# Score visits of three pieces in batches 1 and 2, and narrower dummy matmuls before batch 0's first scores

## The chip, the core and the metric

The kernel runs on one core of one Trainium2 chip. The core has engines that work side by side, each through its own queue in the order in which the instructions were written: TensorE (in the profile PE, with its weight loads as PEld) multiplies matrices into PSUM banks; VectorE (DVE) and ScalarE (ACT) do elementwise work and are the ones that read PSUM; GpSimd (POOL) casts and issues loads; SyncE (SP) issues loads, transposing transfers and stores. Engines wait for one another through semaphores. The metric is the time of one execution on the device in microseconds.

## The reference

Attention with a few extra "beacon" keys, then a two-layer MLP with a squared ReLU. B, H, S, D = 8, 8, 576, 64 (batches, heads, tokens, width of a head), 16 beacons, and for the MLP 4608 tokens x 512, hidden width 2048:

```python
k_all = np.concatenate([beacon_k, k], axis=2)
v_all = np.concatenate([beacon_v, v], axis=2)
scores = scale * np.matmul(q, k_all.transpose(0, 1, 3, 2))
scores = np.where(causal, -1000000000.0, scores)      # beacons are seen by all tokens
a = softmax(scores)
x = (a @ v_all), the heads of a token side by side    # 4608 x 512
h = x @ w_in
r = np.maximum(h, 0.0)
out = (r * r) @ w_out
```

The inputs and the output are float32; the kernel multiplies in bfloat16.

## The kernel before

**Work.** The eight batches run through attention one after another. In a batch two heads form a pair, four pairs in all. The scores are computed transposed (keys on the partitions, queries along the row), in blocks that leave out what the causal mask removes. For each pair 1664 columns per head are left; the four pairs of a batch are cut into 13 *pieces* of 512 columns per head (`STREAM`, `PIECES`, lines 556 to 575). A piece is computed by TensorE (line 620, the two heads on the two halves of the array's rows), put through an exponential by ScalarE into `pt` (line 629, or line 671 in halves), masked by VectorE (lines 712, 716), multiplied by v on TensorE (line 738, with a column of ones that gives the sum) and normalized by VectorE (lines 755, 757) into `xn`. `xn` is transposed into `xT`, by TensorE for batches 0 to 2 (line 805) and by DMA after that. The MLP takes tokens in nine chunks of 512: the first layer (line 901), the ReLU on ScalarE or VectorE (lines 917, 919), the square on VectorE (line 926), the second layer (line 939; line 851 at the very end), copies out of PSUM and stores. A chunk needs the attention of all its tokens: chunk 0 lies in batch 0, chunk 1 in batches 0 and 1, and so on.

**PSUM.** There are two *strips* (two banks each, a piece for both heads) and four single `ps` banks. The `ps` banks serve the MLP's products, the attention-value products, the transposes and the dummies.

**Score visits.** A *visit* is one stretch in which TensorE computes the scores of several pieces, one after the other. `PLAN` (line 636) gives the sizes of the visits of batches 1 to 7. A visit of two takes both strips. A visit of three takes both strips and two `ps` banks besides: its first piece goes into the two banks, one head each, and its exponential is run as two instructions of 512 columns (line 671); the other two pieces go into the strips and have one exponential of 1024 each (line 629). A visit of three is also written behind the visit before it (line 659). Batch 0 is computed otherwise, per pair in four smaller pieces (`add_pair`).

**Loads.** Batches 0 and 1 have q and k brought by GpSimd's DMA queue directly in bfloat16 (line 449) and transposed by TensorE (lines 481 and 484, copied out to `qT` and `kT` at line 497, by way of the helper at lines 325 and 327). Pair 0 of batch 0 comes first, over `osb`, in two parts (lines 522 and 530). The order on GpSimd's queue is a list (`SOFT`, line 976): pairs 1 to 3 of batch 0, its v, w_in in four quarters, then batch 1's q and k (two pairs at a time), v and w_out. From batch 2 on, SyncE loads, GpSimd casts and SyncE transposes by DMA (line 404).

**The order.** `Order.run` (lines 70 to 199) is a planner that runs while the program is built. Every operation has engines that it may run on, an assumed duration, a priority, dependencies, and the banks or buffers that it takes and gives. The planner runs a clock over these and, each time an engine is free, writes down the available operation of the lowest priority number. The engines later run what was written in that order. Where TensorE has nothing available in the first 22 us of the planner's clock, it writes a *dummy* matmul on zeros (lines 145 to 150, written out at line 295) of 128 or 256 columns, which the planner books at 0.107 us either way. The dummies keep TensorE at work until the first data are there.

The first scores of batch 0 need the first part of pair 0 of q and k: cast (line 530), transposed (line 481), copied out by VectorE, and the beacon keys (lines 416 to 438). In the written order the dummies and the transposes of the second part stand ahead of them.

Of the kernel before, what the change touches and what calls it, by code (L numbers as in the profile page):

```python
# [46 lines left out]
class Order:  # L47
# [22 lines left out]
    def run(self):  # L70
# [9 lines left out]
        def release(op):  # L80
            for e in op.engs:
                avail[e].append(op)
# [11 lines left out]
        now = 0.0  # L94
        while events:
            now = events[0][0]
# [18 lines left out]
            while again:  # L115
                again = False
                for e in engines:
                    if free[e] > now + 1e-9:
                        continue
                    best = None  # L120
                    fallback = None
                    held = False
                    for op in avail[e]:
                        if any(free[x] <= now + 1e-9 for x in op.engs[:op.engs.index(e)]):
                            continue
                        if op.take:
                            pool, cls, need = op.take
                            if len(self.pools[pool]) < need or held and pool == "ps":
                                continue
                            if op.wide and len(self.pools["ps"]) < 2:  # L130
                                continue
                            if cls in self.limits and self.inuse[cls] + need > self.limits[cls]:
                                continue
                        if op.gate is not None and not op.gate(self):
                            if fallback is None or op.prio < fallback.prio:
                                fallback = op
                            continue
                        if op.dma and len(lanes[e]) >= self.DEPTH[e] and lanes[e][-self.DEPTH[e]] > now + 1e-9:
                            continue
                        if best is None or op.prio < best.prio:  # L140
                            best = op
                    if best is None:
                        best = fallback
                    if best is None:
                        if e == "PE" and 0.3 < now < self.FILL_UNTIL and self.pools["ps"]:
                            cols = 128 if now < 4.0 else 256
                            free[e] = now + 0.107
                            issued.append((Op("fill", "PE", 0.107, lambda e, cols=cols, bank=self.pools["ps"][0]: self.fill(bank, cols)), e, now))
                            seq += 1
                            heapq.heappush(events, (free[e], seq, "free", None))  # L150
                        continue
                    op = best
                    started.add(id(op))
                    for u in op.followers:
                        u.left -= 1
                        if u.left == 0:
                            release(u)
                    for ee in op.engs:
                        avail[ee].remove(op)
                    if op.take:  # L160
                        pool, cls, need = op.take
                        op.slots = [self.pools[pool].pop(0) for _ in range(need)]
                        op.held = (pool, cls, op.slots[0])
                        if op.wide:
                            op.wide = [self.pools["ps"].pop(0) for _ in range(2)]
                        if cls in self.inuse:
                            self.inuse[cls] += need
                    dur = op.dur[e] if isinstance(op.dur, dict) else op.dur
                    end = now + dur
                    free[e] = end  # L170
                    self.progress += op.pe_time
                    issued.append((op, e, now))
                    seq += 1
                    heapq.heappush(events, (end, seq, "free", op))
                    if op.dma:
                        dma_free = max(dma_free, now + self.DMA_LAT[e]) + op.dma
                        seen = max(end, dma_free + 1.6)
                        lanes[e].append(seen)
                        seq += 1
                        heapq.heappush(events, (seen, seq, "free", op))  # L180
                    else:
                        seen = end + self.LAT[e]
                    seq += 1
                    heapq.heappush(events, (seen, seq, "done", op))
                    seq += 1
                    heapq.heappush(events, (seen + op.late, seq, "done_pe", op))
                    if op.give is not None:
                        seq += 1
                        heapq.heappush(events, (seen, seq, "give", op))
                    again = True  # L190
# [12 lines left out]
def kernel(  # L203
# [429 lines left out]

    exps_of = {}
    SHIFT = 0.25
    PLAN = ((2,2,2,2,2,2,1),(2,2,2,2,2,2,1),(2,3,3,3,2),(2,3,3,3,2),(2,3,3,3,2),(2,3,3,3,2),(2,3,3,3,2))
    FREE = 2
    last_qk = []

    def add_batch(b):  # L640
# [3 lines left out]
        n = 0  # L644
        for size in PLAN[b - 1]:
            pos = HP * b + 512.0 * n / PW
            box = {}
            runs = [(0,), (1, 2)] if size == 3 else [tuple(range(size))]
            for k, run in enumerate(runs):
                def emit(e, run=run, n=n, box=box, size=size):  # L650
                    for s in run:
                        if size == 3 and s == 0:
                            emit_scores(b, PIECES[n], [ps[x] for x in box["qk"].wide])
                        else:
                            st = strips[box["qk"].slots[s - (size == 3)]]
                            emit_scores(b, PIECES[n + s], [st[:, 0, :], st[:, 1, :]])

                qk = add(f"qk{b}.{n + run[0]}", "PE", 0.2 / len(runs) + 512 * len(run) / 2400.0, emit,
                         prio=-1.0e6 if k else 100.0 * pos - 1000.0, behind=[qk] if k else last_qk[-1:] if size == 3 or b > FREE else [],
                         take=None if k else ("strip", "strip", min(size, 2)), gate=None if k else gate_at(pos - SHIFT))  # L660
# [410 lines left out]
```

## Time and profile before

| | |
|---|---|
| median of 5 runs | 339.14 us (338.79 to 339.21) |
| the profiled execution | 339.21 us, span of its instructions 337.5 us |
| TensorE busy | 333.0 us (99%) |
| ScalarE, VectorE, GpSimd busy | 193.6, 164.1 and 91.7 us |
| the MLP's two layers on TensorE (lines 901, 939) | 74% of the chain that ended last |
| attention-value products (738), scores (620), dummies (295) | 9%, 8%, 3% of that chain |
| exponentials of 1024 columns and the like (629) | 92, 1004 ns each |
| exponentials of 512 columns (671) | 30, 598 ns each |
| dummies | 32 of 128 columns, 51 of 256 |

A line of the profile names the engine, the line of the kernel, the instruction, its output and inputs, shapes, how many (x12) and, in brackets, how long the engine was idle before it and whose work ended the wait. Times are microseconds from the start of the span unless marked ns. A matmul's length in the timeline includes its way through the array, which the next one overlaps; how fast a row of matmuls goes is read from where they start, or from the chain, in which each piece ends where the next begins. The score rows say `strip` or `ps` for where the result goes; in a visit of three the `ps` rows come first.

### The profile page before, as it was taken

Reading aid. Unit: us, or ns where it says so; the run is one execution under the profiler, and the core shown is the slowest. Engines: PE = TensorE matmul, PEld = TensorE weight load, DVE = VectorE, ACT = ScalarE, POOL = GpSimd, SP = SyncE. Lnnn points to the kernel's source line nnn. Section 1 sums busy time; section 2 is a strip of 40 time slices with the busy share of each in tenths; the row PEclk is TensorE's granted clock in tenths of the full one; section 3 lists DMA queues with packets and bytes.
Section 4 is the critical chain, followed back from the end, with each engine's and each line's share of the span. In section 5 each row is a group of like instructions: output and inputs, shape, how many; then the busy total and the mean of one; then the engine's idle time right before and its main releaser. Section 6 shows DMA issues by size and latency. Waiting matters only on the chain.

```text
span 337.5 us, 7825 instructions
## 1 busy us (share of the span) xinstructions
PE 333.0 (99%) x3197; PEld 188.2 (56%) x3197; DVE 164.1 (49%) x384; ACT 193.6 (57%) x290; POOL 91.7 (27%) x145
## 2 busy tenths in 40 slices
PE   8999999999999999999999999999999999999996
PEld 7578766544554555545458845554555544444444
DVE  3786977147465982477117823574247303301400
ACT  3886765377647846566567556676557216515611
POOL 9874803315404604051144032404000000000000
PEclk9999999999999999999999999999999999999999
DMA  8999989999999999899799968998210221011003
GB/s 152 194 207 219 204 145 210 224 244 210 197 206 246 172 194 182 187 232 180 144 242 242 200 134 181 247 195 152 74 62 2 45 89 62 0 64 62 0 15 113
DMA packets 143956, 51.74 MB, mean 153 GB/s; under 512 B 130703, under 2 KB 138799, under 8 KB 143919
## 3 DMA queue, kind: packets, MB, share of 16 engines
q1 hardware_dynamic: 135375, 42.19, 61.4%
q0 software_dynamic: 7904, 8.69, 15.0%
q8 instruction: 25, 0.41, 0.5%
q10 hardware_dynamic: 639, 0.36, 0.4%
q14 instruction: 13, 0.10, 0.1%
HBM read 37.22 MB, written 9.44 MB: 138 GB/s over the span
## 4 chain that ended last, share of the span: by engine, by line
PE 99%; ACT 0%; DVE 0%; issue 0%
PE ps L901 38%; PE ps L939 36%; PE ps L738 9%; PE strip L620 7%; PE ps L295 3%; PE ps L484 1%; PE ps L620 1%; PE ps L805 1%; PE ps L851 1%; PE ps L481 0%; PE ps L429 0%; ACT osb L325 0%; DVE g L301 0%; DVE warm L302 0%
## 5 line engine op out<-in xcount | busy, mean ns | idle before, releaser
L901 PE MATMUL ps<-xT,w_in 128*128 128x512 bf16 (+3 forms) x704 | 134.5, 340 | 0.0
L939 PE MATMUL ps<-w_out,g 128*128 128x512 bf16 x560 | 130.8, 379 | 0.0
L629 ACT ACTIVATE pt<-strip 128x1024 bf16<-128x1024 f32 (+3 forms) x92 | 87.4, 1004 | 22.6 <-PE strip L620 22.2
L901 PEld LDWEIGHTS <-w_in 128*128 128x128 bf16 x704 | 65.3, 98 | 51.5 <-issue 0.9
L917 ACT ACTIVATE g<-ps 128x512 bf16<-128x512 f32 (+2 forms) x119 | 66.9, 562 | 45.2 <-PE ps L901 44.5
L926 DVE TENSOR_TENSOR g<-g 128x1024 bf16<-128x1024 bf16 (+2 forms) x80 | 52.6, 665 | 67.3 <-ACT g L917 66.4
L939 PEld LDWEIGHTS <-g 128*128 128x128 bf16 x560 | 51.2, 98 | 55.8 <-issue 1.7
L327 POOL CAST qk_area<-stg 128x512 bf16<-128x512 f32 (+2 forms) x60 | 40.2, 679 | 62.5 <-DMA stg<-in_k_dram 35.3
L325 ACT COPY osb<-ps 128x512 f32<-128x512 f32 (+2 forms) x34 | 19.3, 571 | 58.0 <-PE ps L939 54.7
L327 POOL CAST vb<-stg 128x512 bf16<-128x512 f32 (+1 forms) x40 | 25.2, 638 | 71.5 <-DMA stg<-in_v_dram 53.5
L738 PEld LDWEIGHTS <-pt 128*128 128x128 bf16 (+1 forms) x960 | 36.4, 98 | 11.0 <-issue 0.6
L738 PE MATMUL ps<-vb,pt 128*128 128x65 bf16 (+1 forms) x960 | 39.4, 194 | 0.0
L712 DVE TENSOR_TENSOR pt<-pt,tri 128x512 bf16<-128x512 bf16 x64 | 28.6, 455 | 19.7 <-ACT pt L671 10.0
L757 DVE TENSOR_TENSOR xn<-ps,rcp 128x320 bf16<-128x320 f32 (+2 forms) x64 | 31.5, 492 | 2.4
L919 DVE TENSOR_SCALAR g<-ps 128x512 bf16<-128x512 f32 (+2 forms) x41 | 24.0, 603 | 14.2 <-PE ps L901 14.0
L620 PEld LDWEIGHTS <-kT 64*128 64x128 bf16 x596 | 19.4, 94 | 17.7 <-issue 16.1
L755 DVE RECIPROCAL rcp<-ps 128x5 f32<-128x5 f32 (+2 forms) x64 | 12.2, 191 | 34.7 <-PE ps L738 34.2
L620 PE MATMUL strip<-qT,kT 64*128 64x112 bf16 (+15 forms) x506 | 29.0, 239 | 0.0
L671 ACT ACTIVATE pt<-ps 128x512 bf16<-128x512 f32 x30 | 16.3, 598 | 6.4 <-PE ps L620 5.2
L327 DVE COPY osb<-ps 128x512 f32<-128x512 f32 (+1 forms) x4 | 2.4, 591 | 23.0 <-PE ps L851 11.7
L295 PE MATMUL ps<-g 128*128 128x256 bf16 (+1 forms) x83 | 11.7, 298 | 1.1 <-DVE warm L302 1.1
L371 POOL DMA_DIRECT2D stg<-in_v_dram x10 | 8.8, 886 | 5.2 <-DMA w_in<-in_moe_w_in_dram 3.8
(42 smaller groups left out, 95.2 us busy)
## 6 DMA issues: line engine op xcount, KB each, us to landing
out_dram<-osb SPq DMA_DIRECT2D x17, 512.0 KB, 4.2
stg<-in_q_dram SPq DMA_DIRECT2D x24, 256.0 KB, 5.0
stg<-in_k_dram SPq DMA_DIRECT2D x18, 256.0 KB, 4.8
stg<-in_v_dram SPq DMA_DIRECT2D x18, 256.0 KB, 4.6
w_in<-in_moe_w_in_dram POOLq DMA_DIRECT2D x4, 512.0 KB, 7.7
w_out<-in_moe_w_out_dram POOLq DMA_DIRECT2D x4, 512.0 KB, 11.2
stg<-in_v_dram POOLq DMA_DIRECT2D x6, 256.0 KB, 8.0
stg<-in_k_dram SPq DMA_DIRECT2D x6, 224.0 KB, 4.4
```

Of the source, the lines that this page charges most:

```text
L295: nc.tensor.matmul(ps[bank][:, 0:cols], g[1][:, 0, 0:128], g[1][:, 0, 0:cols], start=True, stop=True)
L327: eng[e].tensor_copy(dst, src)
L620: nc.tensor.matmul(st[hj][:, at:at + t1 - t0], kT[b % 2][hp, pr, 128 * c:128 * c + 128], qT[b % 2][hp, pr, t0:t1], start=True, stop=True,)
L629: nc.scalar.activation(pt[:, :, at:at + width], strips[qk.slots[s]][:, :, 0:width], AF.Exp, bias=0.0, scale=scale)
L712: nc.vector.tensor_tensor(out=d, in0=d, in1=tri[:, m0:m0 + m, :][:, None].to_broadcast([128, 2, m, 128]), op=ALU.min)
L738: nc.tensor.matmul(a[:, at + (t - tl[0]) * (D + 1):at + (t - tl[0] + 1) * (D + 1)], P[0:rr, hj, o:o + 128], vb[b % 2][0:rr, c, 2 * pr + hj ...
L757: nc.vector.tensor_tensor(out=xn[b % 2].rearrange("p t (h d) -> p h t d", d=D)[:, h0:h0 + nh, tl[0]:tl[0] + nt], in0=a[:, :, :, 0:D], in1= ...
L901: nc.tensor.matmul(h[:, lo - spans[0][0]:hi - spans[0][0]], w_in_sb[:, mc, ft * 128:(ft + 1) * 128], xT[:, mc, lo % RING:lo % RING + hi - lo],
L917: nc.scalar.activation(dst, h, AF.Relu, bias=0.0, scale=1.0)
L919: nc.vector.tensor_scalar(out=dst, in0=h, scalar1=0.0, scalar2=None, op0=ALU.max)
L926: nc.vector.tensor_tensor(out=d, in0=d, in1=d, op=ALU.mult)
L939: nc.tensor.matmul(o, G[:, fc, ts * 128:(ts + 1) * 128], w_out_sb[:, fc, :], start=(fc == 0), stop=(fc == NFT - 1))
```

## The change

Two numbers of the plan change. Dummies are 128 columns wide until the planner's clock reads 7.0 instead of 4.0. The visits of batches 1 and 2 become (2, 2, 3, 3, 3) instead of (2, 2, 2, 2, 2, 2, 1); the pieces are the same 13.

```diff
                         if e == "PE" and 0.3 < now < self.FILL_UNTIL and self.pools["ps"]:
-                            cols = 128 if now < 4.0 else 256
+                            cols = 128 if now < 7.0 else 256
                             free[e] = now + 0.107
...
     SHIFT = 0.25
-    PLAN = ((2,2,2,2,2,2,1),(2,2,2,2,2,2,1),(2,3,3,3,2),(2,3,3,3,2),(2,3,3,3,2),(2,3,3,3,2),(2,3,3,3,2))
+    PLAN = ((2,2,3,3,3),(2,2,3,3,3),(2,3,3,3,2),(2,3,3,3,2),(2,3,3,3,2),(2,3,3,3,2),(2,3,3,3,2))
     FREE = 2
```

## The prediction

> **What bounds the kernel now.** I read the page's busy shares and its chain first, then the chain in order of time, then TensorE's timeline of the first 10 us with the other engines' beside it, last the landing of single loads.
>
> ```profile
> PE 333.0 (99%) x3197; PEld 188.2 (56%) x3197; DVE 164.1 (49%) x384; ACT 193.6 (57%) x290; POOL 91.7 (27%) x145
> ...
> PE 99%; ACT 0%; DVE 0%; issue 0%
> ```
>
> TensorE is busy 99% of the span, and the chain that ended last is TensorE alone. So only less streaming, fewer dead spots inside its stream, or an earlier start shorten the time. The chain in order of time (start, length, what) shows the dead spots:
>
> ```profile
> 65.58 0.86 PE ps L939 x4
> ...
> 78.32 0.55 PE strip L620 x12
> ...
> 105.67 0.33 PE ps L620 x6
> 105.99 0.44 PE strip L620 x12
> ...
> 123.79 2.59 PE ps L939 x12
> ...
> 129.57 2.69 PE ps L939 x12
> ...
> 306.41 13.81 PE ps L901 x64
> ```
>
> 64 matmuls of 512 columns take 13.81, one 0.216. Twelve take 2.59 when attention-value products follow (123.79), but 2.69 when a score visit follows: entering a visit costs 0.10. A visit of two pieces takes 0.55; the two heads of a piece stream side by side, so its columns need 2 x 0.216 = 0.43, and leaving costs 0.12. A visit of three (105.67 with 105.99) takes 0.77 for 0.65 of columns: again 0.12. So **a visit costs 0.22 us beside its columns, whatever its size.**
>
> The other place is the start. TensorE's timeline, and the same rows cut at 6.28:
>
> ```profile
> 5.25 2.30 PE L295 MATMUL ps<-g 128*128 128x256 bf16 x15
> 7.38 0.46 PE L481 MATMUL ps<-ident,qk_area 112*128 112x112 bf16 x6
> 7.78 0.33 PE L620 MATMUL strip<-qT,kT 64*128 64x240 bf16 x4
> ```
> ```profile
> 5.25 1.21 PE L295 MATMUL ps<-g 128*128 128x256 bf16 x5
> ```
> ```profile
> 6.08 1.47 PE L295 MATMUL ps<-g 128*128 128x256 bf16 x11
> ```
>
> VectorE and ScalarE, the first things that follow (in brackets the idle time before):
>
> ```profile
> 7.88 0.51 DVE L327 COPY kT<-ps 128x336 bf16<-128x336 bf16 x1 [1.64 <-PE ps L481]
> ```
> ```profile
> 8.15 0.78 ACT L629 ACTIVATE pt<-strip 128x736 bf16<-128x736 f32 x1 [2.84 <-PE strip L620]
> ```
>
> Between 5.25 and 7.38 TensorE does nothing but 15 dummies. The inputs of the transposes at 7.38 were ready at 5.83 (VectorE's cast, 5.48 to 5.83), those of the first scores at 6.25 (copy of qT, 5.85 to 6.25). **The dummies themselves hold up the first scores**, and ScalarE, which then runs exponentials nearly without a pause to 18.3, starts late.
>
> **The change, part one: the dummies.** The order planner books 0.107 us for a dummy of either width, so the number and places of the dummies stay as they are; only columns change. By the planner's own durations its clock starts dummies at 0.45; 32 of them, transposes (0.27) and the beacon's (0.25) bring it to about 4.4, 15 dummies to 6.0, transposes (0.38) and first scores (0.35) to 6.73. So the 15, and some three of the four after the first scores, fall below 7.0 and shrink. The fifth dummy starts at 6.08, so four took 0.83, about 0.21 each; the eleven from 6.08 to 7.38 are one of 0.21 and ten of 0.109. The clock doubled at 6.29. (The granted clock reads 1.00 throughout; the spacing tells.) Before 4.51 the 128-column dummies came every 0.106. After the change: one at 5.25 that is followed in 0.08, as the first of all was, nine more up to 6.29, and five at half of 0.109, 0.28 in all: transposes at 6.57 instead of 7.38, **0.81 earlier**, first scores at 6.97, above the bound of 6.25. Three of the next four give 0.16 more: 0.97.
>
> The Trainium skill, "TensorE: Matmul & The Clock Gate", section "What's actually happening", says that a monitor lifts the half clock after a busy window of about 3.4 us, and that this window runs freely, so the moment differs between runs by some half a microsecond. Here the doubling comes 5.2 us after the first dummy, which fits a window that began on its own; by the rule a later moment would raise the gain of the 15 dummies towards 1.6 us, which the loads named next would cut to the same 0.5. The page's closing table ("Why this matters for your kernels") warns of idle gaps over about 3 us, after which the clock halves again, and so speaks against shorter dummies; one such window at half clock would cost about 1.7 us and turn the sum into a small loss. TensorE has no gap above 0.2 us in these rows.
>
> The 0.97 cannot all reach the end, because TensorE runs into loads that do not move (the page's DMA row stands at 8 or 9 tenths from the start to beyond 140 us). Pair 3's q of batch 0 is issued at 8.48 and lands 6.2 later, 14.7; its transposes start at 15.45, slack 0.7. Then batch 1's last q load (issued 21.17) and the transposes that need it, TensorE's timeline:
>
> ```profile
> qk_area<-in_q_dram POOLq DMA_DIRECT2D x1, 288.0 KB, 12.7
> ```
> ```profile
> 34.17 0.70 PE L484 MATMUL ps<-ident,qk_area 96*64 96x96 bf16 x24
> ```
>
> It lands at 33.83, and of these 24 the twelve of q start at 34.41, after twelve of k: slack 0.58, less 0.06 from landing to start. So **0.5 us survives**; the rest becomes a short wait there. These loads are issued by GpSimd behind w_in and wait for no matmul. Bounds: 0 (another engine takes it) and 0.97; I take 0.5, the tightest row.
>
> **Part two: the visits.** Batches 1 and 2 go from seven visits each to five: four visits fewer x 0.22 = **0.88 us** on the chain. The columns stay. The first two visits of batch 1 (33.6, 38.1) are the same as before, so the order on every queue is unchanged until about 41 us. Six visits become three-piece ones. Each replaces one exponential of 1024 (about 0.98 in a run) by two of 512 (1.08 for both, at 106.2): 0.1 x 6 = 0.6 us on ScalarE, which between 33 and 102 us is idle a third of the time or more except in 33 to 45 (9.45 of 12 busy) and 65 to 81 (11.5 of 16). Cost 0 while that idle time lasts, 0.6 without it. No DMA is added; stores and loads of SyncE and GpSimd keep their dependencies, batch 2's transposed q and k land at 70.9 against a first use at 75.0, and w_out's last quarter at 49.5 against 51.1.
>
> What is added as a wait: a three-piece visit needs both strips and two of the four ps banks free together, and must follow the visit before it. Behind it on TensorE's queue stand the first-layer blocks, which want the same banks, and on ScalarE their ReLUs, then behind 3.0 us of exponentials instead of 1.94. In batches 3 to 7 fifteen such visits stand beside the same blocks without a pause of TensorE (4.42 for 20 matmuls after 106.4). In 41 to 45 us it is tighter: VectorE is busy 10.85 of the 12 us from 33 to 45. Bound for that one visit: VectorE alone serves a block of 272 in 0.44 plus 0.2 of squaring, TensorE makes one in 0.46; over 3.0 us it falls 1.8 blocks behind, 0.85 us, if no second-layer block fills in. The other bound is 0 (24 matmuls ran through two exponentials at 38.7 in 2.88, 0.03 over their columns). I take 0.1, nearer to that row. The reordering after 41 us may also join or split neighbours: four entries at 0.1 either way, taken as 0.
>
> **Sum.** The profiled execution took 339.21 (span 337.5 and 1.7 around it): 339.21 - 0.5 - 0.88 + 0.1 = 337.9. It lies 0.07 above the median of 339.14, within the spread of 0.42.
>
> **Rivals.** (1) *The early gain is lost*, in the waits of rows 15.45 and 34.17 or on VectorE before 45; only the visits count: 339.1 - 0.88 + 0.1 = 338.4 (338.1 to 338.7). For it: VectorE's load; against it: the slack of 0.5 is there in the rows. (2) *More than forecast*: neighbours join too (0.4) or batch 0's loads land earlier: 337.3. (3) *The shorter dummies free less*, if the clock is up before 5.3: then 15 take 1.6 now and 0.8 after, the first scores come against their bound of 6.25, and 0.7 is left, still more than the 0.5 that the load lets through; where more goes, it falls in with (1). (4) *Slower: TensorE runs dry before chunk 1.* Its first matmuls (64.7) need all of batch 1's attention, and only one block of 0.86 (row 65.58) is left of chunk 0 then. The last visit of batch 1 is at 54.27 now. If three-piece visits wait long for two banks at once, it comes later, and beyond 0.86 every microsecond is idle. To end 0.2% slower it must eat 1.3 + 0.7 + 0.86, thus start after 57.1. The visits at 105.6, 110.8 and 115.2 stand 4.4 to 5.2 apart, which from 41.5 puts the last at 51 to 52, earlier than now. At 8.5 apart it would start at 58.5: 3.4 idle, 339.2 + 3.4 - 1.4 = 341.2. (5) *The same stall in small*: 1 us of it cancels most: 338.9.
>
> **How the numbers follow.** Forecast 337.9 (own range 337.4 to 338.4) 0.60; (1) with (3) 0.16, half of it over the bound; (2) 0.07; (5) 0.08, no measurable change; (4) 0.09. A measurement of this kernel tells 0.2%, 0.7 us, from no change: faster is below 338.46. Faster 0.60 + 0.09 + 0.07 = 0.76, same 0.07 + 0.07 = 0.14, slower 0.10. The range 337.2 to 339.0 leaves out (4) and the ends of (2) and (5).
>
> **What will show it.** In the changed profile: the 15 dummies end near 6.6 and the first exponential starts near 7.35; the transposes near 33.9 wait for the load; batches 1 and 2 have five visits each, the exponentials of 512 (line 671) go from 30 to 42; the chain holds no piece but TensorE's; the last visit of batch 1 lies before 54. Wrong would be: TensorE idle after 41 us, above all before chunk 1's first matmuls, or dummies that end as late as now.

## The result and the profile after

| | before | after |
|---|---|---|
| median time | 339.05 us (48 runs) | 338.13 us (27 runs) |
| ratio, 95% interval | 1 | 0.9977 (0.9968 to 0.9986) |
| span of the profiled execution | 337.5 us | 336.5 us |
| TensorE busy | 333.0 us | 331.4 us |

The kernel became 0.8 us faster by the ratio, 0.9 by the medians. The forecast was 337.9, a gain of 1.2. The sign was right and the size a third to a half too large, and one of the two parts gave next to nothing, as the profile and the experiments show. The page's chain by engine, which was TensorE alone before:

```profile
PE 89%; DMA 6%; POOL 4%; issue 0%; ACT 0%; POOLq 0%
```

Where the transfers stand in it, the chain in order of time says (start, length, what):

```profile
6.10 0.82 POOL stg L371
6.92 6.85 DMA stg<-in_v_dram
...
17.75 1.42 POOL w_in L830 x2
19.17 1.97 POOL qk_area L449 x3
21.14 13.39 DMA qk_area<-in_q_dram
34.57 0.45 PE ps L484 x12
```

Up to 34.5 us the end now hangs on GpSimd's queue and on two loads; TensorE enters the chain only with the transposes of the load that the prediction had named. TensorE's own timeline of the same execution:

```profile
5.25 1.41 PE L295 MATMUL ps<-g 128*128 128x128 bf16 x15
6.50 0.46 PE L481 MATMUL ps<-ident,qk_area 112*128 112x112 bf16 x6
6.89 0.33 PE L620 MATMUL strip<-qT,kT 64*128 64x240 bf16 x4
...
14.49 0.45 PE L484 MATMUL ps<-ident,qk_area 96*64 96x96 bf16 x12 [0.68 <-DMA qk_area<-in_k_dram]
...
33.99 1.03 PE L484 MATMUL ps<-ident,qk_area 96*64 96x96 bf16 x24
...
38.23 0.62 PE L620 MATMUL strip<-qT,kT 64*128 64x96 bf16 x12
```

The first scores come at 6.89 instead of 7.78, and the second visit of batch 0 at 8.24 instead of 9.29, 1.05 earlier. At 14.49 TensorE waits 0.68 for pair 3's k. The 24 transposes at 33.99 take 1.03 where they took 0.70, because q lands in their middle. Batch 1's second visit then starts at 38.23, where it was at 38.09 before: **the whole second won at the start is gone.** Three loads took it, each of which landed later than in the profile before:

| load | landed before | landed after | TensorE's lead behind it |
|---|---|---|---|
| (none yet; second visit of batch 0) | | | 1.05 |
| pair 3's k of batch 0 | 13.89 | 14.45 | 0.30 |
| batch 1's first k | 29.34 | 29.85 | 0.18 |
| batch 1's last q | 33.83 | 34.53 | -0.12 |

Matmul by matmul the lead falls at these three places and at no other before 38 us, and 0.75 of the 1.05 goes at pair 3's k. The rest of the span, from batch 1's second visit on, is 298.3 instead of 299.4: this is where the time was won. The rows of the profile before for it:

```profile
38.09 0.62 PE L620 MATMUL strip<-qT,kT 64*128 64x96 bf16 x12
38.64 2.95 PE L901 MATMUL ps<-xT,w_in 128*128 128x272 bf16 x24
...
64.56 1.03 PE L901 MATMUL ps<-xT,w_in 128*128 128x512 bf16 x4
65.42 1.03 PE L939 MATMUL ps<-w_out,g 128*128 128x512 bf16 x4
```

The 24 matmuls at 38.64 take 2.79 in the profile after, and as much with the dummies alone and with the wide dummies below, which have the old visits here. So 0.15 of the 1.1 is a pause that this one execution of the kernel before had. The visits of three in batch 1, TensorE's timeline after the change:

```profile
41.51 0.39 PE L620 MATMUL ps<-qT,kT 64*128 64x192 bf16 x6
41.74 0.60 PE L620 MATMUL strip<-qT,kT 64*128 64x224 bf16 x12
46.32 0.39 PE L620 MATMUL ps<-qT,kT 64*128 64x192 bf16 x4
46.55 0.61 PE L620 MATMUL strip<-qT,kT 64*128 64x144 bf16 x14
54.44 0.40 PE L620 MATMUL ps<-qT,kT 64*128 64x208 bf16 x6
54.67 0.60 PE L620 MATMUL strip<-qT,kT 64*128 64x272 bf16 x12
```

### The profile page after: what moved, and what is told of

Read it like the earlier page. It is cut to its first block, busy times and chain, and to the rows that moved or that the text cites. A ratio compares the mean times of both kernels' runs of the same rounds, so it can differ in the third digit from the quotient of the medians.

```text
span 336.5 us, 7856 instructions
## 1 busy us (share of the span) xinstructions
PE 331.4 (99%) x3197; PEld 188.6 (56%) x3197; DVE 170.4 (51%) x389; ACT 191.2 (57%) x291; POOL 92.1 (27%) x145
## 4 chain that ended last, share of the span: by engine, by line
PE 89%; DMA 6%; POOL 4%; issue 0%; ACT 0%; POOLq 0%
PE ps L939 36%; PE ps L901 36%; PE ps L738 8%; PE strip L620 5%; DMA qk_area<-in_q_dram 4%; PE ps L620 2%; DMA stg<-in_v_dram 2%; POOL qk_area L449 1%; PE ps L851 1%; POOL w_in L830 1%; POOL vb L327 1%; PE ps L805 1%; PE ps L484 0%; POOL tri L311 0%; POOL stg L371 0%; POOL stg L370 0%
## 5 line engine op out<-in xcount | busy, mean ns | idle before, releaser
L629 ACT ACTIVATE pt<-strip 128x1024 bf16<-128x1024 f32 (+3 forms) x86 | 81.4, 1004 | 13.2 <-PE strip L620 13.0
L325 ACT COPY osb<-ps 128x512 f32<-128x512 f32 (+2 forms) x29 | 16.4, 568 | 65.2 <-PE ps L939 60.5
L712 DVE TENSOR_TENSOR pt<-pt,tri 128x512 bf16<-128x512 bf16 x64 | 29.7, 472 | 12.3 <-ACT pt L629 6.7
L919 DVE TENSOR_SCALAR g<-ps 128x512 bf16<-128x512 f32 (+2 forms) x42 | 24.7, 605 | 13.2 <-PE ps L901 12.3
L671 ACT ACTIVATE pt<-ps 128x512 bf16<-128x512 f32 x42 | 22.8, 597 | 13.7 <-PE ps L620 11.1
L620 PE MATMUL strip<-qT,kT 64*128 64x208 bf16 (+13 forms) x474 | 27.0, 239 | 0.0
L327 DVE COPY osb<-ps 128x512 f32<-128x512 f32 (+1 forms) x9 | 5.8, 647 | 33.9 <-PE ps L939 22.1
L295 PE MATMUL ps<-g 128*128 128x128 bf16 (+1 forms) x83 | 10.7, 287 | 1.1 <-DVE warm L302 1.1
```

The lines of the kernel that those rows point to most:

```text
L327: eng[e].tensor_copy(dst, src)
L620: nc.tensor.matmul(st[hj][:, at:at + t1 - t0], kT[b % 2][hp, pr, 128 * c:128 * c + 128], qT[b % 2][hp, pr, t0:t1], start=True, stop=True,)
L629: nc.scalar.activation(pt[:, :, at:at + width], strips[qk.slots[s]][:, :, 0:width], AF.Exp, bias=0.0, scale=scale)
L671: nc.scalar.activation(pt[:, hj, at:at + 512], ps[qk.wide[hj]], AF.Exp, bias=0.0, scale=scale)
L712: nc.vector.tensor_tensor(out=d, in0=d, in1=tri[:, m0:m0 + m, :][:, None].to_broadcast([128, 2, m, 128]), op=ALU.min)
L919: nc.vector.tensor_scalar(out=dst, in0=h, scalar1=0.0, scalar2=None, op0=ALU.max)
```

## The experiments

Theory: up to about 50 us the stream of loads on GpSimd's queue sets the pace, so that an earlier start of TensorE only lengthens its waits; after that TensorE's own stream sets the time, and the visits shorten it. Rival A: half a microsecond of the earlier start survives. Rival B: the gain comes from the start, and the visits are paid back.

**Each part alone.** The dummies alone (this diff and those of the next three kernels are against the kernel before, the later ones against the changed kernel, and they show what is new):

```diff
-                            cols = 128 if now < 4.0 else 256
+                            cols = 128 if now < 7.0 else 256
```

> The dummies' change alone, visits as before. Theory (the loads set the pace of the first 35 us): first scores near 6.9 instead of 7.8, then TensorE waits for a load of q or k, near 14 or near 34 us, and by batch 1's second visit (38.1 before) it is no more than 0.3 us earlier; time 338.8 to 339.1, within 0.1% of before. Rival A (0.5 us of the earlier start survives, as the prediction had it): second visit at 37.6, time about 338.5, ratio 0.9985.

Ratio to the kernel before 1.0001 (0.9982 to 1.0019). Its timeline:

```profile
5.26 1.78 PE L295 MATMUL ps<-g 128*128 128x128 bf16 x15
6.83 0.59 PE L481 MATMUL ps<-ident,qk_area 112*128 112x112 bf16 x6
7.35 0.33 PE L620 MATMUL strip<-qT,kT 64*128 64x240 bf16 x4
...
16.40 0.45 PE L484 MATMUL ps<-ident,qk_area 96*64 96x96 bf16 x12 [1.01 <-DMA qk_area<-in_q_dram]
```

In this execution the clock rose later, so that all 15 dummies took 0.105 us each; the first scores still came 0.43 earlier than before, and a wait of 1.01 at 16.40 took it back. The loads were late here too, and the second visit of batch 1 starts at 39.30; this execution is one of the longer ones of its kernel (340.33, the median is 339.00). The interval of the time (0.6 us to each side) would hold rival A's 0.5 as well; it is the waits that speak against it.

The visits alone:

```diff
-    PLAN = ((2,2,2,2,2,2,1),(2,2,2,2,2,2,1),...
+    PLAN = ((2,2,3,3,3),(2,2,3,3,3),...
```

> The visits alone, dummies as before. Theory (each visit costs two changes of TensorE's row mode at 0.097, four visits fewer are eight changes fewer, 0.78, and one short pause near 40.3 goes): time 0.8 to 0.9 below before, ratio 0.9975, the same as the whole change within 0.1%. Rival A (both parts add): 0.8 below before, and the whole change 0.4 to 0.5 better than this. Rival B (the gain lies in the earlier start, visits are paid back by more work on ScalarE): ratio 0.999 to 1.000.

Ratio 0.9984 (0.9961 to 1.0007), median 338.22, within 0.1 us of the whole change; its profiled span of 336.4 and second visit at 38.16 are those of the whole change. From the second visit on it takes 298.2. TensorE waits for no load in it, and its chain is TensorE's: with the old dummies it came just in time. In these two executions the narrower dummies turned work on zeros into waiting and nothing else.

**Dummies made wider**, to move TensorE's start the other way:

```diff
-                            cols = 128 if now < 4.0 else 256
+                            cols = 128 if now < 4.0 else 512 if now < 7.0 else 256
...
-    nc.vector.memset(g[1][:, 0, 0:256], 0.0)
+    nc.vector.memset(g[1][:, 0, 0:512], 0.0)
```

> Dummies of 512 columns where the change has 128 (between 4.0 and 7.0 of the planner's clock), visits as before: TensorE's start is moved the other way. First scores near 9.5 instead of 7.8 by twice the cost per dummy (five more at the slow clock, the rest at 0.216), some 1.9 later with the three after them. Theory (elastic up to the slack before the loads, stiff beyond): of 1.9 us the slack of 0.6 is taken up, 1.2 to 1.5 reach the end; time 340.3 to 340.6, while 1 us earlier brought nothing. Rival A (start moves the end one to one): 341.0. Rival C (loads hide the start wholly): 339.1.

Ratio 1.0055 (1.0038 to 1.0072), 1.9 us longer, at the upper end of what was expected. The interval includes rival A's 341.0, and in this direction the trace sides with rival A: first scores at 9.03, 1.25 later than before, batch 0's second visit 1.56 later, batch 1's second visit at 39.66, 1.57 later, and no wait for a load. The expectation reckoned the slack of 0.6 the wrong way round. Slack before a load is eaten by being early; whoever comes later than the load pays all of it.

**Small visits in all batches:**

```diff
-    PLAN = ((2,2,2,2,2,2,1),(2,2,2,2,2,2,1),(2,3,3,3,2),...
+    PLAN = ((2,2,2,2,2,2,1),) * 7
```

> Visits of (2, 2, 2, 2, 2, 2, 1) in all seven batches: ten visits and twenty changes of row mode more than before. Theory (0.097 for each change, nothing else on TensorE's path): 20 x 0.097 = 1.9 us longer, 341.0, ratio 1.0057. Rival B (visits of three are dear in other ways, so that small ones are not worse): 339.1 or less. Rival D (small visits also bring stalls by the strips): over 342.

Ratio 1.0062 (1.0047 to 1.0076), 2.1 us for ten visits and twenty changes of the array's form: 0.10 for each change, 0.21 for a visit. Rivals B and D fall.

**One load more**, the same data fetched twice:

```diff
+                if i == 0:
+                    nc.gpsimd.dma_start(out=w_out_sb[:, 0:4, :], in_=moe_w_out.rearrange("(c p) f -> p c f", p=128)[:, 0:4, :])
                 return [nc.gpsimd.dma_start(
```

> The changed kernel with one load more on GpSimd's queue ahead of w_in (w_out's first quarter, 1 MB of float32, which is loaded again at its usual place); nothing else moves, no engine computes more. Theory (the stream of loads sets the pace up to the last of w_out, near 50 us): all later loads land about 2.5 us later (the four quarters of w_in land 2.5 to 3.3 apart), TensorE, which has no slack at batch 1's last q load, waits that long, and time rises by 2.2 to 2.7: 340.3 to 340.8. Rival A (TensorE's own stream sets the time and the waits at loads are chance): under 0.7.

Ratio to the kernel before 1.0049 (1.003 to 1.0069), which is 0.7% or 2.4 us over the changed kernel, as the theory had it, though no engine computes more and the order is the same. Its timeline (lines after 830 are shifted by two) shows where:

```profile
23.61 0.58 PE L903 MATMUL ps<-xT,w_in 128*128 128x240 bf16 x4 [0.52 <-DMA w_in<-in_moe_w_in_dram]
29.25 1.97 PE L903 MATMUL ps<-xT,w_in 128*128 128x240 bf16 x16 [0.85 <-DMA w_in<-in_moe_w_in_dram]
32.77 0.70 PE L484 MATMUL ps<-ident,qk_area 96*64 96x96 bf16 x24 [1.55 <-DMA qk_area<-in_k_dram]
```

The last q of batch 1 lands 2.9 later than after the change alone (37.44), the span is 2.7 longer and the time 2.4: a later load counts nearly in full. These seven kernels share the written order up to batch 1's second visit, and their profiled executions can be set side by side (the landing is the issue of batch 1's last q load plus its time to landing):

| kernel | q lands | second visit | landing to visit | visit to end of span |
|---|---|---|---|---|
| before | 33.83 | 38.09 | 4.26 | 299.4 |
| dummies alone | 35.60 | 39.30 | 3.70 | 299.3 |
| wide dummies | 34.59 | 39.66 | 5.07 | 299.0 |
| visits alone | 34.43 | 38.16 | 3.73 | 298.2 |
| the whole change | 34.53 | 38.23 | 3.70 | 298.3 |
| one load more | 37.44 | 41.14 | 3.70 | 298.1 |
| small visits everywhere | 34.89 | 38.60 | 3.71 | 301.2 |

In four of seven the visit starts 3.70 to 3.71 us after the landing, with the old dummies (small visits) as with the narrow ones; the visits alone, with the old dummies, touch that bound. Only where TensorE is later (before, wide dummies) does it set the time itself. The last column depends, to within 0.4, on the visits alone. And the landing moves by 1.8 us between executions whose loads are the same (without the one with a load more): the execution from which the slack of 0.58 was read had the earliest of them.

**Giving the early start somewhere to go.** If TensorE waits for batch 1's load, its transposes should stand later in the order:

```diff
-                    after = [add_part_load(b, 0, prs, x, prio + n, after, [], 1.5, 1.5)]
+                    after = [add_part_load(b, 0, prs, x, prio + n, after, [], 1.5, 3.5)]
```

> The changed kernel, with the planner told that batch 1's q and k loads are seen 2 us later (1.5 becomes 3.5): TensorE's transposes of them are written four first-layer blocks (16 matmuls, about 1.9 us) later; nothing else before them moves. Theory (after the change TensorE waits for the landing of batch 1's last q load): no wait between 29 and 36 us, three changes of row mode fewer (0.3), time 0.5 to 0.9 below the changed kernel's 338.1, about 337.4. Rival A (that load is passed anyway, the early gain goes elsewhere): only the 0.3 of the row mode, 337.8 or more.

338.28, ratio 0.9977 (0.9958 to 0.9995): no better than the change, so the expectation failed, and rival A's 337.8 or more held. The wait at 34 is gone, but others have taken its place:

```profile
10.07 0.45 PE L484 MATMUL ps<-ident,qk_area 96*64 96x96 bf16 x12 [0.78 <-DMA qk_area<-in_k_dram]
49.72 1.02 PE L939 MATMUL ps<-w_out,g 128*128 128x512 bf16 x3 [0.88 <-DMA w_out<-in_moe_w_out_dram]
```

At 10.07 TensorE stands before pair 2's k of batch 0, at 49.72 before w_out's last quarter. The same kernel with the old dummies:

> The same as the one before with the old dummies (256 columns from 4.0 on); the written order is the same. Theory: with the load at 34 us out of the way the dummies count as far as the first load, pair 3's k near 14 us, lets them: 0.2 to 0.5 us longer than with the narrow dummies, though the same pair without this edit differed by nothing. Rival A (the early start is lost somewhere else): equal. Rival E (nothing else in the way): 1.0 longer.

338.87, ratio 0.9989 (0.9973 to 1.0005). The medians differ by 0.6 from the narrow dummies, but the intervals overlap, and here w_out landed later (51.0), which again is what ended the wait. With pair 3's load moved ahead of v as well:

```diff
-    SOFT = "t0 p1k p1q t1 p2k p2q v0 v1 p3k p3q v2 v3 v4 w0 w1 w2 w3".split()
+    SOFT = "t0 p1k p1q t1 p2k p2q p3k p3q v0 v1 v2 v3 v4 w0 w1 w2 w3".split()
```

> The changed kernel with the late transposes of the first run and, besides, pair 3's k and q of batch 0 loaded ahead of v instead of behind two of its loads, so that the wait near 14 us goes too. Theory: TensorE's early second of the dummies passes both places; 0.3 to 0.8 below the late transposes alone, about 336.8. Rival F (v then lands too late for the first attention-value products, and the wait only moves): equal or slower.

337.93, ratio 0.9965 (0.9952 to 0.9979), no clear step; and with the old dummies:

> The same as the one before with the old dummies, the written order the same. Theory: with both loads out of the way the dummies are worth what they free at the start, 0.7 to 1.05 us: about 337.7 against 336.8. Rival A: equal. Rival F: a difference under 0.3, because v's landing holds both.

338.15, ratio 0.9971 (0.9957 to 0.9985). The dummies' 0.7 to 1.05 did not appear in the medians, which lie 0.2 apart. (The two profiled executions say little of it: the first scores came at 7.02 and 7.23, because the clock rose earlier in the second.) Both stand before w_out, here the kernel with the narrow dummies and then the one with the old:

```profile
49.49 1.02 PE L939 MATMUL ps<-w_out,g 128*128 128x512 bf16 x3 [0.72 <-DMA w_out<-in_moe_w_out_dram]
```
```profile
49.80 1.02 PE L939 MATMUL ps<-w_out,g 128*128 128x512 bf16 x3 [0.66 <-DMA w_out<-in_moe_w_out_dram]
```

**The last load of the stage.** In the kernel with both edits and the narrow dummies, the planner was told besides that w_out is seen late, by 4 us (5 in a second kernel):

```diff
-            w_ops["out", i] = add(..., behind=[v_loads[1][4]] if i == 0 else [w_ops["out", i - 1]], dma=2.6)
+            w_ops["out", i] = add(..., behind=[v_loads[1][4]] if i == 0 else [w_ops["out", i - 1]], dma=2.6, late=4.0)
```

> The kernel with pair 3 loaded early and batch 1's transposes late, and the planner told besides that w_out's loads are seen 4 us later. There TensorE waited 0.9 us for w_out's last quarter (landed 49.45). Theory: with that wait gone, 0.5 to 0.9 below it, 337.1 to 337.4. Rival G (the work put ahead is missing later, and TensorE waits at another place up to chunk 1's start): 337.9 or more.

> The same with 5 us instead of 4, which writes batch 1's attention-value products ahead of the second layer's first block. Theory: 337.1 to 337.4 as with 4. Rival G: 337.9 or more.

340.68 and 341.02, ratios 1.0043 (1.0026 to 1.0061) and 1.0054 (1.0036 to 1.0072): slower than the kernel before, as rival G had it. The first of them:

```profile
59.76 0.39 PE L620 MATMUL ps<-qT,kT 64*128 64x208 bf16 x6
...
63.44 0.43 PE L805 MATMUL ps<-ident,xn 112*128 112x112 bf16 x5 [0.95 <-DVE xn L757]
64.30 1.27 PE L738 MATMUL ps<-vb,pt 128*128 128x65 bf16 x30 [0.43 <-DVE pt L712]
66.54 0.43 PE L805 MATMUL ps<-ident,xn 112*128 112x112 bf16 x5 [0.97 <-DVE xn L757]
66.81 6.44 PE L901 MATMUL ps<-xT,w_in 128*128 128x512 bf16 x27
```

The last visit of batch 1 slid to 59.76, and before chunk 1 (66.81) TensorE ran dry three times, 2.35 us together. This is the mechanism of the prediction's fourth rival, brought about by another cause. With 2 us instead of 4 the planner writes one other block between, and the visits hardly move:

> The kernel with pair 3 loaded early and batch 1's transposes late, and w_out's loads taken to be seen 2 us later instead of 4: the block that needs w_out's last quarter is written 1.3 us later, the visits of batch 1 at most 0.9 later. Theory: the wait for w_out (0.7 to 0.9 there) goes and, as the last visit of batch 1 stays before 54.4, no wait takes its place before chunk 1: ratio to the kernel before 0.994 to 0.995, about 337.2. Rival G (as with 4 and 5 us, TensorE runs dry before chunk 1): 0.997 or more.

337.21, **ratio 0.9949 (0.9932 to 0.9966), span 334.9**, better than both kernels: its interval ends just below that of the change. Between 5 and 75 us one wait of TensorE is left:

```profile
10.81 0.45 PE L484 MATMUL ps<-ident,qk_area 96*64 96x96 bf16 x12 [0.18 <-DMA qk_area<-in_k_dram]
...
51.51 0.40 PE L620 MATMUL ps<-qT,kT 64*128 64x208 bf16 x6
...
63.54 2.75 PE L901 MATMUL ps<-xT,w_in 128*128 128x512 bf16 x12
```

The last visit starts at 51.51 and chunk 1 at 63.54. Before the change a block of chunk 0's second layer still stood behind chunk 1's first block (the row at 65.42 above); here none is left, so that like for like chunk 1 comes 1.9 earlier. Not all of this is the early start: the late transposes save three changes of the array's form besides, about 0.3. No run with the old dummies stands beside this kernel, so what the narrow ones are worth in it is not shown.

## Why the prediction was right, and where it was not

*The total.* 337.9 against 338.1 is in part luck. The sum held a gain of 0.5 from the start, 0.88 from the visits and a loss of 0.1. In the profiled executions the start gave -0.1 and everything behind batch 1's second visit 1.1. A term that did not come was half made up by one that came out larger and by a loss that did not show. The sign "the chain holds no piece but TensorE's" failed too: 6% of it are loads and 4% GpSimd.

*The visits, 0.88.* Right: five visits in each of the two batches, 42 exponentials of 512 columns instead of 30, and the price of 0.22 per visit held: 0.21 from the small visits everywhere, and 0.7 to 1.3 from the last column of the table for four visits (299.0 to 299.4 against 298.1 to 298.3). Eight changes of form at 0.10 are 0.8 of it, and 0.15 of the difference between the profiles before and after is the pause at 38.64; the rest was not traced. The Trainium skill, "TensorEngine Tiling (Array Packing)", section "Key Properties", says that changing the tiling mode drains TensorE, without a figure. The runs put a change at 0.10 us each way; that draining is the cause no run here shows.

*The start, 0.81 and 0.97.* Right as far as it goes: 0.89 and 1.05 in the profile after. The moment of the clock is not fixed. The dummies' spacing puts it at 6.29 before, near 6.15 after, later than 6.83 with the dummies alone, near 7.0 with the late transposes and the old dummies, and in the profile of the small visits the first 256-column dummies at 4.96 were already 0.109 apart. With w_out 4 us late the first 32 dummies take 3.22 instead of 3.59, which puts it near 3.8. The Trainium skill, "TensorE: Matmul & The Clock Gate", section "What's actually happening", gives half a microsecond to each side; these executions, whose first 32 dummies are the same, lie 3.2 us apart, and the measurement decides.

*"So 0.5 us survives".* **This is the step that failed.** The right load was named, the first loss at pair 3 too (it came at pair 3's k, which the prediction did not read: landed 13.89, transposes at 14.79), but the slacks of 0.7 and 0.58 came from one execution, and for batch 1's last q that had the earliest landing of six. In the others q lands 0.6 to 1.8 later, TensorE is bound to it with the old dummies already or nearly so, and what is won ahead of it turns into waiting. The dummies alone measured 0.0 (ratio 1.0001, 0.6 us to either side), the lower of the two bounds that the prediction had set; the time by itself would still allow 0.5, and the waits and the table rule it out only for the profiled executions. Rival 1, in its form for the waits at the loads, had the mechanism. The time does not choose: 338.1 lies midway between its 338.4 and the forecast's 337.9.

*The stall, 0.1.* None showed beside the visits of three: no row of TensorE between 38 and 61 us of the profile after has a wait in it. The row that the prediction took as nearly undisturbed, 24 matmuls at 38.7 in 2.88, "0.03 over their columns", was 0.15 over: the same 24 take 2.73 from start to start after the change.

*The last visit of batch 1 before 54.* Wrong: 54.44, since the last two visits of three stand 8.1 apart, not 4.4 to 5.2. Chunk 1 starts at 65.03 with TensorE busy up to it and nothing of chunk 0 left; before it was 64.56, or 65.42 with the block that stood behind its first four matmuls. So rival 4 lay nearer than the spacing of later batches suggested, and the runs with w_out late crossed over to it: a visit at 59.8 cost 2.35 us of idle TensorE, where the prediction had put 3.4 for one at 58.5.

*The chances.* Added up from the list of rivals they give 0.75, 0.16 and 0.09; the last line has 0.76, 0.14 and 0.10.

## What to carry to other kernels

An engine that is busy 99% of the time can still hang on another one's pace, or stand half a microsecond from it, when part of its work before a load is filler: ask of each stage not how busy it is but what the next fixed landing is, and take slack from several executions, not from one. In these runs work pulled ahead of a landing brought nothing measurable until every landing of that stage had other work written in front of it, one after the other (pair 3, batch 1's q, w_out), and each such shift has its own far side, where the next stage runs dry. How much of the last gain is the early start's was not separated. Fewer changes of the array's form, by contrast, paid at once, because they stand where TensorE alone sets the time.

## What was not expected of the hardware

The landing of the same load at the same place in the queue moved from 33.83 to 35.60 us between executions, and in most of them everything behind it moved along. Of these 1.8 us, GpSimd's issue makes 1.0 (21.17 to 22.21) and the way from issue to landing 0.7 (12.7 to 13.4). The time of the kernel before spread over 338.1 to 340.6 in 48 runs; that the landings make that spread fits the table, but was not shown run by run, and the moment of the clock, which moved TensorE's start by as much, may have a share in it.
